# Two S4D convolutions around routed-token layers: the convolution kernel becomes the stationary operand of its spectrum's first stage, ScalarE instead of VectorE moves the result, and D_skip enters by small matmuls

## The chip, the cores and the metric

One NeuronCore of one Trainium2 chip runs the whole program; the other cores are idle. The metric is the device time of one execution in microseconds (us), smaller is better. The engines are named as in the profile: PE (TensorE; PEld is its weight loading), DVE (VectorE), ACT (ScalarE), POOL (GpSimd) and SP (SyncE, whose queue issues nearly all DMAs). Each engine takes its own instructions strictly in the order in which the program lists them, and waits at an instruction until the semaphores that it needs have come.

## What is computed

Four layers follow each other, with residual connections: a convolution layer A, a routed layer B, A again and B again. The sequence has L = 2048 positions and D = 512 channels, all in float32. A is a diagonal state-space model. It builds for each channel a kernel K of 2048 taps out of N = 128 complex states, and convolves the normalized input with it by FFT:

```python
dt = jnp.exp(log_dt)
A = -jnp.exp(log_A_real) + 1j * A_imag
C = (C_real + 1j * C_imag) * dt[:, None]
P = jnp.exp((A * dt[:, None])[:, :, None] * pos[None, None, :])
K = 2.0 * jnp.einsum("dn,dnl->dl", C, P).real
Kf = jnp.fft.rfft(K, 2 * L)
Uf = jnp.fft.rfft(u_t, 2 * L)
y = jnp.fft.irfft(Uf * Kf, 2 * L)[:, :, :L]
return y + u * D_skip
```

Both A layers have the same parameters, so K and its spectrum are computed once. B sends two tokens of the sequence through a SwiGLU network and leaves the rest as it is.

## The kernel before

The channels go in 4 chunks of 128. The kernel K is made in 32 steps of 16 channels, 8 steps for each chunk; `KStep` (L434) is such a step, and `slot(t)` (L722) writes out one slot of a software pipeline in which five steps are under way at a time. In a slot, POOL computes integer phases (`phase`, L454) and decays (`decay`, L465 and L467) by doubling, ACT turns phases into sines and cosines (`trig`, L474 to L476), and DVE and POOL multiply the decays into them (`products`, L482 to L489). PE then contracts over the 128 states (`contract`, L497): 32 matmuls with 32 stationary columns and 64 moving ones fill the PSUM tile `pk`, with 4 channel groups `g` side by side in four column strips of the array. A float32 matmul shows in the profile as two instructions. ACT copies `pk` to the SBUF tile `kt` (L499).

The first stage of K's spectrum is a transform over the 32 coarse positions of each tap, and it is here that the change works. `spectrum` (L501) first adds D_skip to tap 0 of 16 channels by a 128x4 instruction of DVE (L503), out of a tile `dskt` that has a value in partitions 0, 32, 64 and 96 and zeros elsewhere. Then 8 matmuls (L507) hold the constant `d1k` stationary (64 columns) and move `kt`, read with a stride, so that the result `kq` has frequencies on its partitions and (position, channel) on its free axis. `turn` (L514) brings the positions to the partitions by one DVE instruction that transposes blocks of 32x32 (L517) and writes into `gk`, the chunk's input of the second stage.

The second stage (`kf2`, L533 or L524: `kx`) multiplies `gk` by the constant `w2`, ACT copies the result to `kd` (L540), and SP stores it in DRAM as `kfd` (L542). Beside the pipeline, the first convolution of the chunks that are ready runs: `load` reads `kfd` back (`kf`, L561), `f1` transforms the input (PE `zf` L593, DVE transpose `g` L597), `front` multiplies the spectra (PE `pu` L533, DVE `p` L568), `back` transforms back (PE `pv` L579, ACT `v` L580), `fin_a` and `fin_b` finish (DVE `vt` L638, PE `po` L640, DVE `xc` L647), and `stats` (L653, L654) takes the statistics for the next layer. The table `CONV1` names by hand, in thirds of a slot, where each of these pieces stands in program order.

What sets the order: in the slots from 6 to 31 the program order of DVE, ACT and POOL is kept as written (`ORDER_KERNEL`, L136, by `in_order`, L210). The order of PE's instructions and of SP's DMAs there, and the order of all engines in the opening before slot 6, is chosen by a scheduler that weighs ready times by a model of its own. The opening also holds the setup of the state parameters and the statistics of the first normalization. The buffers of the pipeline come in pairs (`KB` = 2): decays `mg`, phases `ph` and sines `sc` of a step can be begun again only when the step two before has used them up. `mg`'s first column is written by ACT (`decay_init`, L459), which so waits until `products` of the step two before are done. There is one `gk` buffer (tag `bigC`) for all chunks; in slots 9, 17 and 25 the `turn` is therefore held back to the next slot's start.

Of the kernel before, what the change touches and what calls it, by code (L numbers as in the profile page):

```python
# [8 lines left out]
F32 = mybir.dt.float32  # L9
# [5 lines left out]
OP = mybir.AluOpType  # L15
# [14 lines left out]
PP = 2  # L30
# Where each step of the work beside the kernel's pipeline, and of what follows it, stands in program order.
CONV1 = dict(
# [110 lines left out]
def constants():  # L143
# [5 lines left out]
    for s in range(2):  # L149
        for h in range(2):  # L150
            d1[s, h, :, s, h, 0, :] = np.cos(th)
            d1[s, h, :, s, h, 1, :] = -np.sin(th)
    d1k = np.zeros((4, 32, 4, 2, 32))
    for g in range(4):
        d1k[g, :, g, 0, :] = np.cos(th)
        d1k[g, :, g, 1, :] = -np.sin(th)
    d4 = np.zeros((2, 2, 32, 2, 32))
    for h in range(2):
        d4[h, 0, :, h, :] = np.cos(th.T) / 2048.0
        d4[h, 1, :, h, :] = -np.sin(th.T) / 2048.0  # L160
    b = np.arange(64)
# [4 lines left out]
    for h in range(2):  # L166
        sl = slice(32 * h, 32 * h + 32)
        w2[h, 0, :, :, 0, :] = c[sl]
        w2[h, 1, :, :, 0, :] = s[sl]
        w2[h, 0, :, :, 1, :] = -s[sl]  # L170
        w2[h, 1, :, :, 1, :] = c[sl]
    w2 = w2.reshape(128, 32, 128)
# [37 lines left out]
@contextmanager  # L210
def in_order(tc, engines):
    """Instructions traced in the block keep their order on each of these engines."""
    seen = tc.nc.cur_bb.bb.instructions
    n = len(seen)
    yield
    prev = {}
    for i in seen[n:]:
        if i.engine in engines:
            if i.engine in prev:
                dep = mybir.DependencyInfo(mybir.DependencyClass.NoSync, mybir.DependencyReason.DATA)  # L220
                tc.add_manual_dep(i, prev[i.engine].name, dep, reason="in_order")
            prev[i.engine] = i


def build(tc, x, lar, aim, cr, ci, ldt, dsk, wr, wg, wu, wd, d1_h, d1k_h, d4_h, w2_h, w3_h, w3b_h, sm_h, out):
# [6 lines left out]
    with ctx:  # L232
# [39 lines left out]
        d1k = kp.tile([128, 256], F32, name="d1k", tag="d1k")  # L272
        dskt = kp.tile([128, 32, 4], F32, name="dskt", tag="dskt")
        LN2H, LN2L = 0.693145751953125, 1.42860682030941723e-06
# [49 lines left out]
        def setup(c0, c1, room):  # L324
            """Phases and decays of a state's powers: plane k holds those of step 2^(k-1), as (coarse, fine) pairs."""
            n = (c1 - c0) * CH
# [107 lines left out]
        class KStep:  # L434
            """Sixteen channels of the kernel and of its spectrum's first stage, in steps."""

# [54 lines left out]
            def contract(self):  # L491
                pk = psk.tile([128, 4, 64], F32, name=f"pk{self.u}", tag="pk")
                for e in range(4):
                    for k in (1, 0):
                        for g in range(4):
                            t = self.sc[:, k, 4 * g + e, :]
                            T.matmul(pk[32 * g : 32 * g + 32, e, :], t[:, 0:32], t[:, 33:97], start=k == 1, stop=k == 0, tile_position=(0, 32 * g))  # L497
                self.kt = kp.tile([128, 4, 64], F32, name=f"kt{self.u}", tag="kt", bufs=2)
                A.activation(self.kt, pk, AF.Copy)  # L499

            def spectrum(self):  # L501
                kt = self.kt
                V.tensor_tensor(kt[:, :, 32], kt[:, :, 32], dskt[:, self.u, :], op=OP.add)  # L503
                self.pq = psk.tile([128, 32, 16], F32, name=f"kq{self.u}", tag="kq")
                for g in range(4):
                    for h in range(2):
                        T.matmul(  # L507
                            self.pq[64 * h : 64 * h + 64, :, 4 * g : 4 * g + 4],
                            d1k[:, 64 * g : 64 * g + 64],
                            kt[:, :, 32 - 32 * h : 64 - 32 * h].rearrange("p e b -> p b e"),  # L510
                            start=True, stop=True, tile_position=(0, 64 * h),
                        )

            def turn(self):  # L514
                if self.s == 0:
                    gks[self.c] = new_big(f"gk{self.c}", "C")
                V.transpose(gks[self.c][:, :, 16 * self.s : 16 * self.s + 16].rearrange("p k e -> p e k"), self.pq.rearrange("p b e -> p e b"))  # L517

# [25 lines left out]
        def kf_pair(c, gi):  # L544
            """Spectra of two groups, even k1 on the lower partitions and odd ones on the upper."""
            kf = sb.tile([128, 2, 2, 2, CH], F32, name=f"kf1_{c}_{gi}", tag="kf", bufs=2)
# [157 lines left out]
        nc.sync.dma_start(d1k, d1k_h)  # L704
        G.memset(dskt, 0.0)
        for g in range(4):
            nc.sync.dma_start(dskt[32 * g : 32 * g + 1].rearrange("p s e -> p (s e)"), dsk[g : g + 1, :])
        def merged(chain, lanes, plan):
            """The chain's steps, with those of each lane put in before the step that the plan names."""
            todo = sorted(((p, k, lane) for lane, ps_ in plan.items() for k, p in enumerate(ps_)), key=lambda w: (w[0], w[2], w[1]))  # L710
# [9 lines left out]
        def slot(t):  # L720
            """One step of the kernel's pipeline; other work may come after any of its instructions."""
            def at(k, f, *a):  # L722
# [77 lines left out]
        class Conv:  # L800
            """One chunk of a convolution layer, in steps."""

# [172 lines left out]
        class Routed:  # L975
            """The layer of the two routed tokens, in steps, and the next convolution's start beside it."""

# [23 lines left out]
            def choose(self):  # L1001
                """Statistics, scores, the two tokens and their normalized rows."""
                i, rdt, small, psum = self.i, self.rdt, self.small, self.psum
# [428 lines left out]
```

## Time and profile before

| | |
|---|---|
| Time of the runs | 697.32 us median of 3 (696.2 to 698.96) |
| Span of the profiled execution | 695.2 us |
| Instructions | 14060 |
| Mean granted TensorE clock | 0.882 |
| Bytes moved by DMA | 97.64 MB, 140 GB/s in the mean |

The span runs from the first to the last instruction that the profiler recorded. The first 43 us hold the opening, the pipeline of the 32 steps runs from there to about 389 us, and the rest is the end of the first convolution, the first routed layer, the second convolution and the second routed layer. Lines of the profile give a group of instructions by source line, engine and operation, `out<-in` by the names of the tiles, the shape, and either the times of one group or the start and length of single pieces. What stands in brackets behind a piece is the time for which its engine had been idle, and what ended that.

### The profile page before, as it was taken

What the parts mean: (1) busy time and instruction counts of PE and PEld (TensorE: products, weight loads), DVE (VectorE), ACT (ScalarE), POOL (GpSimd) and SP (SyncE); (2) the same over time, 40 slices, a digit from 0 to 9 for tenths busy, and PEclk for the clock granted to TensorE, in tenths of its full rate; (3) what the DMA queues carried; (4) which work ended last, traced back from release to release, by engine and by line L of the source; (5) the groups of instructions that cost most, each with busy time, mean ns of one, the idle gap of its engine ahead of it and who ended that gap; (6) DMA issues with size and microseconds to landing.
All of it is one profiled execution on the core that took longest, in us unless ns stands there. A gap on an engine that the chain in (4) does not pass through costs nothing.

```text
span 695.2 us, 14060 instructions
## 1 busy us (share of the span) xinstructions
PE 485.8 (70%) x5300; PEld 360.2 (52%) x5300; DVE 580.9 (84%) x1164; ACT 311.1 (45%) x587; POOL 500.4 (72%) x659
## 2 busy tenths in 40 slices
PE   1012433798988898979789987267799888888336
PEld 1001322577855786648776665034678565656112
DVE  7899998687899999989999964985356799999950
ACT  4445645456753647527473121321511615214272
POOL 4879999999999999987993083260257766757252
PEclk9999775699998989979999998769599899999858
DMA  7961204768410977109460699600813748438436
GB/s 212 225 150 72 90 30 144 262 195 234 118 33 28 218 214 171 53 16 245 117 172 2 184 307 345 164 2 11 178 55 86 154 103 176 145 98 239 108 79 180
DMA packets 51709, 97.64 MB, mean 140 GB/s; under 512 B 4885, under 2 KB 35513, under 8 KB 47161
## 3 DMA queue, kind: packets, MB, share of 16 engines
q1 hardware_dynamic: 51512, 96.72, 51.5%
q8 instruction: 42, 0.69, 0.4%
q14 instruction: 27, 0.21, 0.1%
q0 software_dynamic: 128, 0.02, 0.0%
HBM read 70.23 MB, written 26.48 MB: 139 GB/s over the span
## 4 chain that ended last, share of the span: by engine, by line
DVE 33%; POOL 21%; DMA 16%; PE 14%; issue 8%; SPq 6%; ACT 1%; POOLq 0%; DVEq 0%; ACTq 0%
POOL mg L465 6%; DVE vt L638 6%; POOL ph L454 6%; PE zf L593 4%; DVE g L597 3%; DMA x<-in_x 3%; DVE jn L654 3%; DMA xw<-xs 3%; DVE p L609 3%; SPq L561 3%; DMA kf<-kfd 3%; DMA x<-xs 3%; POOL sc L482 2%; POOL ml L467 2%; DVE p L568 2%
## 5 line engine op out<-in xcount | busy, mean ns | idle before, releaser
L465 POOL TENSOR_TENSOR mg<-mg,pf 128x128 f32<-128x128 f32 (+4 forms) x160 | 108.6, 682 | 5.4 <-ACT pf L423 3.1
L454 POOL TENSOR_TENSOR ph<-ph,pi 128x512 int32<-128x512 int32 (+4 forms) x160 | 112.0, 702 | 0.5
L497 PE MATMUL pk<-sc 128*32 128x64 f32 x2048 | 46.3, 247 | 74.2 <-DVE sc L489 63.5
L618 POOL TENSOR_TENSOR y<-p 64x256 f32<-64x256 f32 x76 | 55.9, 736 | 50.0 <-DVE p L609 35.6
L507 PE MATMUL kq<-kt,d1k 128*64 128x128 f32 x512 | 63.4, 402 | 30.8 <-DVE kt L503 22.5
L593 PE MATMUL zf<-z,d 128*128 128x256 f32 x256 | 80.1, 453 | 5.9 <-DVE g L597 5.1
L497 PEld LDWEIGHTS pk<-sc 128*32 128x32 f32 x2048 | 38.4, 126 | 87.8 <-issue 57.8
L638 DVE STREAM_TRANSPOSE vt<-v 128x512 f32<-128x512 f32 x64 | 69.2, 1098 | 3.3 <-ACT v L626 2.5
L597 DVE STREAM_TRANSPOSE g<-zf 128x512 f32<-128x512 f32 x64 | 65.9, 1051 | 7.0 <-PE zf L593 7.0
L626 ACT ACTIVATE v<-pv 128x512 f32<-128x512 f32 x40 | 23.7, 596 | 97.9 <-PE pv L625 97.9
L593 PEld LDWEIGHTS zf<-z,d 128*128 128x128 f32 x256 | 52.7, 222 | 24.9 <-DVE g L597 11.7
L507 PEld LDWEIGHTS kq<-kt,d1k 128*64 128x64 f32 x512 | 40.1, 159 | 46.7 <-DVE kt L503 25.2
L640 PE MATMUL po<-vt,d 128*64 128x256 f32 x256 | 45.0, 432 | 23.1 <-DVE vt L638 22.6
L619 POOL TENSOR_TENSOR y<-p 64x256 f32<-64x256 f32 x76 | 55.6, 731 | 4.6
L625 PE MATMUL pv<-y,w 128*128 128x128 f32 x320 | 54.8, 302 | 5.0 <-POOL y L619 3.7
L524 PE MATMUL pu<-g,w 128*64 128x128 f32 x640 | 50.2, 298 | 10.2 <-DVE g L1297 3.6
L489 DVE TENSOR_TENSOR sc<-mg,sc 128x1024 f32<-128x1024 f32 x32 | 57.3, 1790 | 0.0
L625 PEld LDWEIGHTS pv<-y,w 128*128 128x128 f32 x320 | 45.1, 201 | 19.6 <-POOL y L619 9.5
L482 POOL TENSOR_TENSOR sc<-mg,sc 128x512 f32<-128x512 f32 x25 | 40.8, 1631 | 12.3 <-ACT sc L476 12.3
L609 DVE TENSOR_TENSOR p<-pu,kf 128x1024 f32<-128x1024 f32 x32 | 38.4, 1209 | 12.8 <-PE pu L524 6.2
L524 PEld LDWEIGHTS pu<-g,w 128*64 128x64 f32 x640 | 38.7, 147 | 18.4 <-DVE p L609 6.2
L579 PE MATMUL pv<-p,w 128*128 128x128 f32 x192 | 40.7, 296 | 7.5 <-DVE p L568 7.1
(344 smaller groups left out, 1175.0 us busy)
## 6 DMA issues: line engine op xcount, KB each, us to landing
kf<-kfd SPq DMA_DIRECT2D x144, 128.0 KB, 4.0
kfd<-kd SPq DMA_DIRECT2D x16, 512.0 KB, 6.8
wd<-in_wd SPq DMA_DIRECT2D x4, 1792.0 KB, 14.0
w<-in_w SPq DMA_DIRECT2D x2, 2048.0 KB, 11.1
x<-in_x SPq DMA_DIRECT2D x8, 512.0 KB
xc<-in_x SPq DMA_DIRECT2D x8, 512.0 KB, 6.0
z<-in_x SPq DMA_DIRECT2D x8, 512.0 KB, 6.4
xs<-xc SPq DMA_DIRECT2D x8, 512.0 KB, 4.3
```

The lines of the kernel that those rows point to most:

```text
L454: G.tensor_tensor(self.ph[:, :, n : 2 * n], self.ph[:, :, 0:n], self.step_of(self.pis, k + 1, n), op=OP.add)
L465: G.tensor_tensor(mg[:, :, n : 2 * n], mg[:, :, 0:n], self.step_of(self.pfs, k + 1, n), op=OP.mult)
L489: V.tensor_tensor(sc[:, :, :, at], m.rearrange("p (o d) i -> p o d i", o=1).to_broadcast([128, 2, 16, 32]), sc[:, :, :, at], op=OP.mult)
L497: T.matmul(pk[32 * g : 32 * g + 32, e, :], t[:, 0:32], t[:, 33:97], start=k == 1, stop=k == 0, tile_position=(0, 32 * g))
L507: T.matmul(self.pq[64 * h : 64 * h + 64, :, 4 * g : 4 * g + 4], d1k[:, 64 * g : 64 * g + 64], kt[:, :, 32 - 32 * h : 64 - 32 * h].rearrang ...
L524: T.matmul(pt[64 * par : 64 * par + 64, ri, q, :], w2[:, k1, 64 * ri : 64 * ri + 64], src[:, k1, :], start=True, stop=True, tile_position= ...
L593: T.matmul(pf[:, 16 * s : 16 * s + 16, :], d1[:, 128 * s : 128 * s + 128], z[:, :, 16 * q : 16 * q + 16], start=True, stop=True)
L597: V.transpose(g[:, :, 16 * q : 16 * q + 16].rearrange("p k e -> p e k"), pf.rearrange("p b e -> p e b"))
L609: V.tensor_tensor(pp, pu.rearrange("p (o r) q e -> p o r (q e)", o=1).to_broadcast([128, 2, 2, 2 * CH]), kf.rearrange("p r (o q) e -> p r ...
L618: E.tensor_tensor(y[0:64, :, par, :], p1[ls, 0], p2[ls, 1], op=OP.subtract)
L625: T.matmul(pv[:, k, :], w3[:, 4 * gi + k, :], y[:, k // 2, k % 2, :], start=True, stop=True)
L638: V.transpose(vt.rearrange("p b e -> p e b"), v[:, :, es].rearrange("p k e -> p e k"))
```

## The change

`contract` adds D_skip on PE: between the two passes over a column of `pk` it puts 4 matmuls of 4 contraction rows, 32 stationary columns (of the constant tile `sm`, of which only column 0 of each strip holds a one) and 1 moving column, which add to tap 0. So L497's 32 matmuls of a step become 48. The DVE addition (L503) goes. `dskt` is now 4 partitions high, loaded by one DMA in place of four, and its clearing by POOL goes.

`spectrum` swaps the operands: `kt` (64 columns, contiguous) is stationary, `d1k` (128 columns, contiguous) moves, and there are 8 matmuls as before. The result has the positions on its partitions already, so `turn` needs no transpose; it is a copy of the 128x512 result by ACT, written into `gk` with a step of 128 elements (512 bytes) from one element to the next. To suit the new order of partitions (real and imaginary part outside, half of the positions inside), the constants `d1`, `d1k`, `d4` and `w2` are permuted, in their values only; no shape of their use changes.

```diff
-        dskt = kp.tile([128, 32, 4], F32, name="dskt", tag="dskt")
+        dskt = kp.tile([4, 32, 4], F32, name="dskt", tag="dskt")
...
             def contract(self):
                 pk = psk.tile([128, 4, 64], F32, name=f"pk{self.u}", tag="pk")
                 for e in range(4):
-                    for k in (1, 0):
+                    for k in (1, None, 0):
                         for g in range(4):
-                            t = self.sc[:, k, 4 * g + e, :]
-                            T.matmul(pk[32 * g : 32 * g + 32, e, :], t[:, 0:32], t[:, 33:97], start=k == 1, stop=k == 0, tile_position=(0, 32 * g))
-                self.kt = kp.tile([128, 4, 64], F32, name=f"kt{self.u}", tag="kt", bufs=2)
-                A.activation(self.kt, pk, AF.Copy)
+                            at, gs = pk[32 * g : 32 * g + 32, e, :], (0, 32 * g)
+                            if k is None:
+                                T.matmul(at[:, 32:33], sm[0:4, 200 + 32 * g : 232 + 32 * g], dskt[:, self.u, e : e + 1], start=False, stop=False, tile_position=gs)
+                            else:
+                                t = self.sc[:, k, 4 * g + e, :]
+                                T.matmul(at, t[:, 0:32], t[:, 33:97], start=k == 1, stop=k == 0, tile_position=gs)
+                self.kt = kp.tile([128, 4, 2, 32], F32, name=f"kt{self.u}", tag="kt", bufs=2)
+                A.activation(self.kt, pk.rearrange("p e (h b) -> p e h b", h=2)[:, :, ::-1, :], AF.Copy)
 
             def spectrum(self):
-                kt = self.kt
-                V.tensor_tensor(kt[:, :, 32], kt[:, :, 32], dskt[:, self.u, :], op=OP.add)
-                self.pq = psk.tile([128, 32, 16], F32, name=f"kq{self.u}", tag="kq")
-                for g in range(4):
-                    for h in range(2):
+                self.pq = psk.tile([128, 4, 4, 32], F32, name=f"kq{self.u}", tag="kq")
+                for e in range(4):
+                    for ri in range(2):
                         T.matmul(
-                            self.pq[64 * h : 64 * h + 64, :, 4 * g : 4 * g + 4],
-                            d1k[:, 64 * g : 64 * g + 64],
-                            kt[:, :, 32 - 32 * h : 64 - 32 * h].rearrange("p e b -> p b e"),
-                            start=True, stop=True, tile_position=(0, 64 * h),
+                            self.pq[64 * ri : 64 * ri + 64, e].rearrange("p g k -> p (g k)"),
+                            self.kt[:, e].rearrange("p h b -> p (h b)"),
+                            d1k[:, 128 * ri : 128 * ri + 128],
+                            start=True, stop=True, tile_position=(0, 64 * ri),
                         )
 
             def turn(self):
                 if self.s == 0:
                     gks[self.c] = new_big(f"gk{self.c}", "C")
-                V.transpose(gks[self.c][:, :, 16 * self.s : 16 * self.s + 16].rearrange("p k e -> p e k"), self.pq.rearrange("p b e -> p e b"))
+                A.activation(
+                    gks[self.c][:, :, 16 * self.s : 16 * self.s + 16].rearrange("p k (g e) -> p e g k", g=4),
+                    self.pq, AF.Copy)
...
-        G.memset(dskt, 0.0)
-        for g in range(4):
-            nc.sync.dma_start(dskt[32 * g : 32 * g + 1].rearrange("p s e -> p (s e)"), dsk[g : g + 1, :])
+        nc.sync.dma_start(dskt.rearrange("p s e -> p (s e)"), dsk)
```

The tables of the program order (`CONV1` and the others) are as before. The scheduler, which sees other instructions, lists some of the rest in another order: in the opening the last steps of DVE's chain that doubles the decays (L426) stand behind statistics of the input (L788); where the second stage of chunk 0 begins, SP's queue has the load of the next input `z` ahead of the stores of `kfd`, and for chunks 1 and 2 the four loads of the first `kf` ahead of the second store of `kfd`, where each stood behind; and PE has `kq` earlier at several places, that of steps 15 and 23 ahead of a finishing tile `po` and three tiles `zf` of the input's transform, where it stood behind them. From the routed layer on, all engines have the same order as before.

More of the change, by code (lines that the diff above doesn't have):

```diff
@@ L150, in constants @@
         for h in range(2):
-            d1[s, h, :, s, h, 0, :] = np.cos(th)
-            d1[s, h, :, s, h, 1, :] = -np.sin(th)
-    d1k = np.zeros((4, 32, 4, 2, 32))
+            d1[s, h, :, s, 0, h, :] = np.cos(th)
+            d1[s, h, :, s, 1, h, :] = -np.sin(th)
+    d1k = np.zeros((4, 32, 2, 4, 32))
     for g in range(4):
-        d1k[g, :, g, 0, :] = np.cos(th)
-        d1k[g, :, g, 1, :] = -np.sin(th)
+        d1k[g, :, 0, g, :] = np.cos(th)
+        d1k[g, :, 1, g, :] = -np.sin(th)
     d4 = np.zeros((2, 2, 32, 2, 32))
     for h in range(2):
-        d4[h, 0, :, h, :] = np.cos(th.T) / 2048.0
-        d4[h, 1, :, h, :] = -np.sin(th.T) / 2048.0
+        d4[0, h, :, h, :] = np.cos(th.T) / 2048.0
+        d4[1, h, :, h, :] = -np.sin(th.T) / 2048.0
     b = np.arange(64)
@@ L167, in constants @@
         sl = slice(32 * h, 32 * h + 32)
[L168 to L171, printed above, removed]
+        w2[0, h, :, :, 0, :] = c[sl]
+        w2[1, h, :, :, 0, :] = s[sl]
+        w2[0, h, :, :, 1, :] = -s[sl]
+        w2[1, h, :, :, 1, :] = c[sl]
     w2 = w2.reshape(128, 32, 128)
```

## The prediction

> **What bounds the kernel now.** I read the engines' totals first, then busy time by stage, then what ended the idle time of the engine that is busy throughout a stage.
>
> ```profile
> PE 485.8 (70%) x5300; PEld 360.2 (52%) x5300; DVE 580.9 (84%) x1164; ACT 311.1 (45%) x587; POOL 500.4 (72%) x659
> ```
>
> The totals name DVE, but the change lies in the pipeline of the 32 steps alone, 43 to about 389 us. The view by windows (busy us of PE, PEld, DVE, ACT, POOL, each with its count) shows who fills it:
>
> ```profile
> 43.00:200.00 157.00, 94.17 (x1408) 77.53 (x1408) 136.86 (x160) 89.65 (x146) 155.50 (x175) 0.84 0.44 138
> 200.00:300.00 100.00, 85.72 (x1142) 65.16 (x1140) 97.68 (x141) 55.13 (x91) 98.67 (x126) 0.93 0.46 119
> 300.00:376.00 76.00, 67.13 (x862) 53.67 (x864) 72.65 (x112) 43.35 (x72) 62.67 (x83) 0.92 0.48 126
> 376.00:400.00 24.00, 22.28 (x272) 15.74 (x268) 23.66 (x63) 2.78 (x5) 0.20 (x1) 1.00 0.48 137
> ```
>
> Up to 300 us POOL is busy 254 of 257 us: whatever DVE sheds there cannot shorten the stage, because POOL's own 32 steps of phases, decays and products are untouched. From 200 us on DVE is full as well (97.68 of 100), and after 300 us POOL falls to 62.67 of 76: something keeps it waiting. The timeline of POOL has these pieces with idle time ahead of them:
>
> ```profile
> 310.30 0.29 POOL L465 TENSOR_TENSOR mg<-mg,pf 128x32 f32<-128x32 f32 x1 [1.52 <-ACT mg L459]
> 320.93 1.99 POOL L482 TENSOR_TENSOR sc<-mg,sc 128x512 f32<-128x512 f32 x1 [4.52 <-ACT sc L476]
> 350.78 1.77 POOL L482 TENSOR_TENSOR sc<-mg,sc 128x512 f32<-128x512 f32 x1 [0.96 <-ACT sc L476]
> 373.32 1.21 POOL L482 TENSOR_TENSOR sc<-mg,sc 128x512 f32<-128x512 f32 x1 [4.54 <-ACT sc L476]
> ```
>
> Together 11.54 us, all of it on ACT's cosines or first columns. ACT is not full (43.35 of 76); its queue stands. The timelines of ACT, DVE and PE before the second of those gaps say for whom:
>
> ```profile
> 309.95 0.27 ACT L459 ACTIVATE mg<-pf 128x32 f32<-128x32 f32 x1 [6.01 <-DVE sc L489]
> 314.25 0.60 ACT L540 ACTIVATE kd<-kx 128x512 f32<-128x512 f32 x1 [4.03 <-PE kx L533]
> 319.66 1.19 ACT L476 ACTIVATE sc<-ph,cst 128x1056 f32<-128x1056 f32 x1
> ```
>
> ```profile
> 307.76 0.29 DVE L503 TENSOR_TENSOR kt<-kt,dskt 128x4 f32<-128x4 f32 x1
> 308.58 1.28 DVE L489 TENSOR_TENSOR sc<-mg,sc 128x1024 f32<-128x1024 f32 x1
> 311.89 1.11 DVE L517 STREAM_TRANSPOSE gk<-kq 128x512 f32<-128x512 f32 x1 [1.10 <-PE kq L507]
> ```
>
> ```profile
> 304.75 5.18 PE L593 MATMUL zf<-z,d 128*128 128x256 f32 x12
> 309.86 1.98 PE L507 MATMUL kq<-kt,d1k 128*64 128x128 f32 x16
> ```
>
> ACT stood 6.01 us because DVE came late to its products, and 4.03 us because `kx` needs `gk`, which needed the transpose (311.89), the matmuls `kq` (309.86) and the addition (307.76), all waiting in DVE's and PE's queues. So a full DVE reaches POOL through ACT. That is the chain which the change cuts.
>
> **The change part by part.** The groups that it touches, or that are like what it adds (busy us, mean ns of one):
>
> ```profile
> L517 DVE STREAM_TRANSPOSE gk<-kq 128x512 f32<-128x512 f32 x32 | 34.5, 1079 | 2.3 <-PE kx L533 1.2 <-PE kq L507 1.1
> L503 DVE TENSOR_TENSOR kt<-kt,dskt 128x4 f32<-128x4 f32 x32 | 14.1, 442 | 8.8 <-ACT kt L499 8.8
> L540 ACT ACTIVATE kd<-kx 128x512 f32<-128x512 f32 x32 | 18.4, 594 | 33.7 <-PE kx L533 14.5 <-PE kx L524 10.8 <-DVE p L609 5.4
> ```
>
> 1. DVE loses 1.08 + 0.44 = 1.52 us a step, 48.6 us in all. About 20 steps of it fall where POOL alone sets the pace (to 300 us) and are worth nothing by themselves, but they let DVE catch up with POOL. In 300 to 376 us about 8 steps fall: 12.2 us less of DVE's 72.65. Bounds of what reaches the end: 0 (POOL's gaps stay) to the 11.54 us of gaps, since POOL's 62.67 us of work remain. Both limits agree on 11 to 12 us; I take 10, as ACT keeps other waits.
>
> 2. ACT gains the copy. The nearest row is L540 (128x512 out of PSUM, 0.594 us), the far one the transpose itself (1.079 us, the same scattered write); 19.0 to 34.5 us in all, I take 0.6 us a step. It is hidden in ACT's idle time (32.6 us of 76). Without this cover, each step would be 0.6 us longer. The copy waits for `kq`; behind it in ACT's queue stand the `kt` copy of the next step, the `kd` and `v` copies, and the next slot's sines, for which POOL waits. But just ahead of it stands L459, which waits for DVE's products of the same slot anyway, and `kq` no longer waits for DVE. Cost 0 here, and a rival below.
>
> 3. PE's `kq`: 16 instructions take 1.98 us with strided operands. The same shape with contiguous ones is this piece:
>
> ```profile
> 392.69 1.09 PE L524 MATMUL kx<-gk,w 128*64 128x128 f32 x16
> ```
>
> So 0.89 us less a step (bounds 0 and 0.89). The 16 small matmuls are 32 instructions between those of `pk`, in another tiling of the array (32x32 in 128x32). How dear that is shows where `pk` is broken up by `po`:
>
> ```profile
> 372.16 0.64 PE L497 MATMUL pk<-sc 128*32 128x64 f32 x26
> 372.73 0.65 PE L640 MATMUL po<-vt,d 128*64 128x256 f32 x4
> 373.31 0.31 PE L497 MATMUL pk<-sc 128*32 128x64 f32 x6
> 373.56 0.65 PE L640 MATMUL po<-vt,d 128*64 128x256 f32 x4
> 381.72 1.10 PE L497 MATMUL pk<-sc 128*32 128x64 f32 x64
> ```
>
> Unbroken, 64 take 1.10 us or 0.017 each; broken, 26 take 0.57 to the next start (0.45 at that pace) and 6 take 0.25 (0.10): 0.12 to 0.15 us for a switch. A switch lies between 0 (should the next weights be in) and 0.15; I take 0.1. Eight switches a step and 32 instructions at 0.017: 0.8 + 0.54 = 1.3 us more, bounds 0.5 and 1.7. With `kq`, +0.4 us a step (-0.4 to +1.7). In 300 to 376 us, 8 steps make 3 us (-3 to +14) on PE's 67.13 of 76, of which 9 are free: cost 0 to the end at the taken value, and 5 us beyond its room at the far one, a rival.
>
> On this the Trainium skill speaks against the change: TensorEngine Tiling (Array Packing), section Tiling Modes, says that changing the tiling mode drains the array. The broken `pk` agrees that there is a price. By a whole passage for each switch, the mean length of a `pk` matmul in the row below, it would be 8 x 0.25 = 2.0 us a step in place of 0.8, and the sum of PE +1.6 in place of +0.4.
>
> ```profile
> L497 PE MATMUL pk<-sc 128*32 128x64 f32 x2048 | 46.3, 247 | 74.2 <-DVE sc L489 63.5 <-POOL sc L486 7.5 <-DVE sc L486 2.5
> ```
>
> 4. The end of the pipeline, 376 to 400 us, is DVE's (23.66 of 24) and PE's (22.28):
>
> ```profile
> 384.17 1.01 DVE L517 STREAM_TRANSPOSE gk<-kq 128x512 f32<-128x512 f32 x1
> 388.48 1.01 DVE L517 STREAM_TRANSPOSE gk<-kq 128x512 f32<-128x512 f32 x1
> ```
>
> Two transposes and two additions (0.26) go, 2.3 us; PE's 1.7 us of slack bounds the gain. I take 2 (0 to 2.3).
>
> 5. The opening. Four DMAs of `dskt` become one and a clearing of POOL goes; POOL's last two waits before its full stretch are
>
> ```profile
> 4.05 1.20 SPq L707 DMA_DIRECT2D dskt<-in_dsk  x4
> 37.26 1.19 POOL L482 TENSOR_TENSOR sc<-mg,sc 128x512 f32<-128x512 f32 x1 [2.27 <-ACT sc L476]
> 41.74 1.31 POOL L359 TENSOR_TENSOR su_bigB<-su_w,su_bigB 128x384 f32<-128x384 f32 x1 [1.86 <-DVE su_bigB L358]
> ```
>
> The inputs are asked for 0.9 us sooner. In the new order POOL does phases first, while DVE's later doublings wait for statistics, and meets DVE's L358 with more work already behind it. Between 4.1 us won (both waits) and 3 lost (waits of this kind anew); I take 1 won.
>
> 6. SP's queue. For chunks 1 and 2 the loads of the first `kf` wait for the first store to land, and the second store is now behind them:
>
> ```profile
> 235.19 2.58 SPq L561 DMA_DIRECT2D kf<-kfd  x4
> ```
>
> ```profile
> 230.38 4.74 DMA kfd<-kd
> ```
>
> ```profile
> 242.74 1.20 ACT L476 ACTIVATE sc<-ph,cst 128x1056 f32<-128x1056 f32 x1
> 249.17 1.24 POOL L482 TENSOR_TENSOR sc<-mg,sc 128x512 f32<-128x512 f32 x1
> ```
>
> The second row is from the chain of waits: a store lands 4.74 us after its issue. So the second store goes out 5 to 6 us later, its buffer is free later, and ACT's third pair of `kd` copies waits for it with the sines behind. POOL has some 5 us in hand at chunk 1 (cosine done at 243.94, its user L482 at 249.17), less at chunk 2. 0 to 5 us; I take 2 lost.
>
> 7. The permuted constants change no instruction: 0. POOL itself may run a little faster: the addition, which reads two SBUF tiles as POOL's work does, took 0.44 us in the mean, but 0.12 while POOL stood:
>
> ```profile
> 379.12 0.12 DVE L503 TENSOR_TENSOR kt<-kt,dskt 128x4 f32<-128x4 f32 x1
> ```
> If each held POOL up for 0.12, 3.8 us; I take 0.
>
> Sum against the profiled execution: 10 + 2 + 1 - 2 = 11 us off 695.2, a span of 684.2. The runs' median, 697.3, lies 2.1 us above the span: **686.3 us**. Its own range, from the bounds of items 1 and 4 to 6 taken mostly one at a time, is 680 to 693.
>
> **The rivals.** (a) *The gaps come back.* ACT's other waits (for `pv`, `pk`, `kx`) take the place of those on DVE; only items 4 and 5 remain: 697.3 - 3 = 694.3, with 1 or 2 us of item 6 against it up to 696. For it: three of the four gaps are 1 us and more on cosines, which only ACT makes. Against: DVE's lateness stood at the root.
>
> (b) *ACT becomes the queue that decides*, on the other side. The copy waits for PE in order, and PE's queue holds `kq` behind tiles that wait for DVE; each time the sines behind it come later than POOL wants them. The margin is already gone where a gap of 0.96 us stands (350.78). The three waits for L476 cost 10.0 us, 3.3 each; if from 200 us on every second step (9 of 17) meets one, 30 us, 20 more than now, less 3 of items 4 and 5: 714. With every third step, 20 us: 704. It decides from the point where `kq` ends later than L459. Against: `kq` leaves DVE's queue.
>
> (c) *PE becomes the bound.* At +1.7 us a step, 17 steps from 200 us make 29 us on PE's 152.9 of 176: 5.8 us too much, none of the 10 us gained, and 3 won elsewhere: 700. By the drained passage of the Trainium skill's page (above), with `kq` saving nothing, it would be 2.5 a step, 43 us, 20 beyond the room: 714. For it: PE is the fullest engine after DVE at the end. Against: `kq`'s strided operands are plainly what makes it slower than L524.
>
> (d) *Everything runs through*: all gaps, the whole of items 4 and 5 and POOL's 3.8: 11.5 + 2.3 + 4.1 + 3.8 = 21.7 us, 676.
>
> **How the numbers follow.** Forecast 0.55, (a) 0.14, (b) 0.15, (c) 0.11, (d) 0.05. What a measurement can tell from no change is 0.5%, 693.8 to 700.8 us. Forecast and (d) are faster, and a little of (a), 0.62; most of (a) and of the lower half of (c) the same, 0.15; the rest slower, 0.23. The range 679 to 704 takes in (a), (c)'s first price and the milder (b); it leaves out (d) and the dearer prices, under 2 in 10.
>
> **What would show it.** Right: POOL's gaps of 4.5 us at 321 and 373 gone, DVE under 90% busy from 200 us, `kq` near 1.1 us, the copy near 0.6 us, and the last `gk` written some 12 us sooner. Item 3 wrong: `pk` beyond 2.8 us. (b): POOL waits for ACT's cosines while ACT waits for `kq`. (c): PE over 95% busy from 200 us. Wrong altogether: POOL's pieces themselves longer, or the pipeline not full at 43 us.

## The result, and the profile after

The changed kernel takes 706.28 us (median of 4 runs, 702.17 to 707.44) beside 697.69 us of the kernel before on the same chip: a ratio of 1.0118, 95% interval 1.0079 to 1.0157. It is slower by 1.2%, where 1.6% faster was forecast. The profiled execution took 707.44 us, with a span of 705.7.

The totals of the engines on the page of the kernel after:

```profile
PE 507.1 (72%) x6324; PEld 382.9 (54%) x6324; DVE 532.8 (76%) x1100; ACT 337.5 (48%) x619; POOL 494.7 (70%) x658
```

DVE lost the 48 us of busy time that the prediction took from it, ACT gained 26 and PE 21. By stages (the windows of the prediction; columns: busy us of PE, PEld, DVE, ACT, POOL, then granted clock, DMA share and GB/s):

```profile
43.00:200.00 157.00, 106.75 (x1837) 86.21 (x1838) 118.15 (x140) 97.60 (x154) 155.66 (x176) 0.82 0.43 138
200.00:300.00 100.00, 89.54 (x1382) 73.13 (x1380) 78.36 (x119) 64.27 (x101) 85.62 (x118) 0.91 0.48 119
300.00:376.00 76.00, 68.63 (x1081) 58.28 (x1080) 61.48 (x96) 45.46 (x76) 66.81 (x85) 0.91 0.48 126
```

To 200 us nothing has changed for POOL: it is as full as before. From 200 to 300 us DVE fell from 97.68 to 78.36, as it should, but POOL fell with it, from 98.67 to 85.62. The engine that set the pace now waits, and no engine is full. The timeline of POOL after 200 us says for what (the larger gaps; in brackets the idle time ahead and what ended it):

```profile
208.13 1.20 POOL L482 TENSOR_TENSOR sc<-mg,sc 128x512 f32<-128x512 f32 x1 [1.23 <-ACT sc L476]
242.03 2.24 POOL L482 TENSOR_TENSOR sc<-mg,sc 128x512 f32<-128x512 f32 x1 [5.88 <-ACT sc L476]
294.94 1.20 POOL L482 TENSOR_TENSOR sc<-mg,sc 128x512 f32<-128x512 f32 x1 [2.04 <-ACT sc L476]
327.94 1.53 POOL L482 TENSOR_TENSOR sc<-mg,sc 128x512 f32<-128x512 f32 x1 [5.44 <-ACT sc L476]
380.19 1.20 POOL L482 TENSOR_TENSOR sc<-mg,sc 128x512 f32<-128x512 f32 x1 [4.43 <-ACT sc L476]
```

The gaps that were to go came back in greater number, and still on ACT's cosines: 21.6 us in seven waits from 43 to 390 us, 10.0 in three before. ACT itself has 35 of 100 us free; what it waits for, and what PE does in the changed lines, stands in the waits of ACT from 43 to 390 us (total us, times, longest) and in the groups by line (busy us, mean ns of one; idle time before them):

```profile
ACT v L585 <- PE pv L584: 33.3, 12, 5.0
ACT kt L503 <- PE pk L501: 18.7, 12, 4.2
ACT gk L520 <- PE kq L510: 2.9, 2, 2.4
```

```profile
L520 ACT ACTIVATE gk<-kq 128x512 f32<-128x512 f32 x32 | 33.9, 1058 | 5.0 <-PE kq L510 5.0
L498 PE MATMUL pk<-dskt,sm 4*32 4x1 f32 x1024 | 32.8, 182 | 0.0
```

ACT's new copy (L520) takes 1.06 us and waits for little. What ACT waits for are PE's old results, `pv` and `pk`. In the kernel before it waited for `pk` even longer:

```profile
ACT kt L499 <- PE pk L497: 32.2, 19, 7.6
```

So these totals alone accuse nobody; what has changed on PE must say more. One step's `kq` and `pk` on PE's timeline of the kernel after:

```profile
192.24 1.09 PE L510 MATMUL kq<-d1k,kt 128*64 128x128 f32 x16
193.26 0.32 PE L501 MATMUL pk<-sc 128*32 128x64 f32 x8
193.51 0.24 PE L498 MATMUL pk<-dskt,sm 4*32 4x1 f32 x8
193.68 0.43 PE L501 MATMUL pk<-sc 128*32 128x64 f32 x16
194.04 0.24 PE L498 MATMUL pk<-dskt,sm 4*32 4x1 f32 x8
...
195.27 0.32 PE L501 MATMUL pk<-sc 128*32 128x64 f32 x8
```

`pk` lasts from 193.26 to 195.59, 2.33 us in place of 1.10 unbroken. `kq` takes 1.09, as predicted. So the suspicion goes to the small matmuls.

### The profile page after: what moved, and what is told of

It is laid out like the page before. It is cut to its first block, busy times and chain, and to the rows that moved or that the text cites. A ratio compares the mean times of both kernels' runs of the same rounds, so it can differ in the third digit from the quotient of the medians.

```text
span 705.7 us, 16088 instructions
## 1 busy us (share of the span) xinstructions
PE 507.1 (72%) x6324; PEld 382.9 (54%) x6324; DVE 532.8 (76%) x1100; ACT 337.5 (48%) x619; POOL 494.7 (70%) x658
## 4 chain that ended last, share of the span: by engine, by line
PE 28%; DVE 27%; DMA 16%; POOL 13%; issue 8%; SPq 5%; ACT 3%; POOLq 0%; DVEq 0%; ACTq 0%
PE pv L584 5%; DVE vt L643 4%; PE pk L501 4%; DVE g L602 4%; PE zf L598 4%; POOL ph L454 3%; DVE jn L659 3%; DMA xw<-xs 3%; POOL mg L465 3%; DMA x<-xs 3%; DVE p L614 3%; DMA xc<-in_x 3%; DMA x<-in_x 3%; DMA kf<-kfd 3%; PE kx L538 2%
## 5 line engine op out<-in xcount | busy, mean ns | idle before, releaser
L501 PE MATMUL pk<-sc 128*32 128x64 f32 x2048 | 72.2, 251 | 64.5 <-DVE sc L489 56.1
L454 POOL TENSOR_TENSOR ph<-ph,pi 128x64 int32<-128x64 int32 (+4 forms) x160 | 111.9, 702 | 3.6 <-ACT ph L448 3.4
L465 POOL TENSOR_TENSOR mg<-mg,pf 128x512 f32<-128x512 f32 (+4 forms) x160 | 109.1, 684 | 7.3 <-ACT pf L423 6.1
L598 PE MATMUL zf<-z,d 128*128 128x256 f32 x256 | 75.4, 430 | 13.1 <-DVE g L602 7.1
L501 PEld LDWEIGHTS pk<-sc 128*32 128x32 f32 x2048 | 42.0, 122 | 75.5 <-issue 62.0
L598 PEld LDWEIGHTS zf<-z,d 128*128 128x128 f32 x256 | 49.1, 209 | 29.0 <-DVE g L602 12.3
L573 DVE TENSOR_TENSOR p<-pu,kf 128x1024 f32<-128x1024 f32 x24 | 28.9, 1218 | 43.2 <-PE pu L538 21.5
L510 PE MATMUL kq<-d1k,kt 128*64 128x128 f32 x512 | 42.7, 320 | 22.2 <-ACT kt L503 22.2
L482 POOL TENSOR_TENSOR sc<-mg,sc 128x512 f32<-128x512 f32 x25 | 36.4, 1455 | 21.6 <-ACT sc L476 21.6
L510 PEld LDWEIGHTS kq<-d1k,kt 128*64 128x64 f32 x512 | 34.8, 162 | 29.4 <-ACT kt L503 24.9
L614 DVE TENSOR_TENSOR p<-pu,kf 128x1024 f32<-128x1024 f32 x32 | 38.4, 1209 | 11.3 <-PE pu L529 4.7
## 6 DMA issues: line engine op xcount, KB each, us to landing
x<-in_x SPq DMA_DIRECT2D x8, 512.0 KB, 10.4
```

Of the source, the lines that this page charges most:

```text
L454: G.tensor_tensor(self.ph[:, :, n : 2 * n], self.ph[:, :, 0:n], self.step_of(self.pis, k + 1, n), op=OP.add)
L465: G.tensor_tensor(mg[:, :, n : 2 * n], mg[:, :, 0:n], self.step_of(self.pfs, k + 1, n), op=OP.mult)
L501: T.matmul(at, t[:, 0:32], t[:, 33:97], start=k == 1, stop=k == 0, tile_position=gs)
L510: T.matmul(self.pq[64 * ri : 64 * ri + 64, e].rearrange("p g k -> p (g k)"), self.kt[:, e].rearrange("p h b -> p (h b)"), d1k[:, 128 * ri ...
L598: T.matmul(pf[:, 16 * s : 16 * s + 16, :], d1[:, 128 * s : 128 * s + 128], z[:, :, 16 * q : 16 * q + 16], start=True, stop=True)
L614: V.tensor_tensor(pp, pu.rearrange("p (o r) q e -> p o r (q e)", o=1).to_broadcast([128, 2, 2, 2 * CH]), kf.rearrange("p r (o q) e -> p r ...
```

## The experiments

Two theories at first. *P*: the small matmuls on PE make the loss, as `pk` is 1.2 us longer in every step. *A*: ACT makes it, with a copy of 1.06 us ahead of the sines. Every time is given as a ratio to the kernel before, measured on the same chip in the same session, with its 95% interval; 1% is 7.0 us.

**e1_no_dskip.** The small matmuls left out, with nothing in their place:

```
-                    for k in (1, None, 0):
+                    for k in (1, 0):
```

> The changed kernel without D_skip: the small matmuls are left out and nothing takes their place, so the output lacks the term D_skip * x. Theory P (PE's small matmuls: pk 1.1 to 2.3 us a step, everything behind them on PE late): the pk matmuls are back at about 1.1 us a step, and the time falls to 690 to 698 us. Theory A (ACT's queue: the scattered copy of 1.06 us a step, with its waits, makes the sines late): the copy is as before, POOL still waits some 20 us for ACT's sines, and the time stays at 703 to 707 us. If both have a part, it lies between.

Measured: 0.9931 (0.9902 to 0.9959), median 691.48 us; POOL has no wait in the pipeline. Theory P's range; the copy on ACT is still there. All that the change loses came with the small matmuls, and without them the rest of it gains. But leaving them out also let the scheduler choose another order, so this run does not yet say whether their execution or that order costs.

**e2_small_alone.** The small matmuls put into the kernel before, DVE's addition taken out:

```
-                    for k in (1, 0):
+                    for k in (1, None, 0):
...
-                V.tensor_tensor(kt[:, :, 32], kt[:, :, 32], dskt[:, self.u, :], op=OP.add)
```

> The kernel before with one part of the change: D_skip enters by the 16 small matmuls a step, DVE's addition is gone; old orientation, transposes on DVE. Theory P: PE is 1.2 us a step later, the DVE addition saves 0.44 us a step on an engine that was full; the time is 702 to 708 us. Theory A: ACT's queue is the old one, so no loss; DVE's relief gives a little, 692 to 698 us.

Measured: 1.0197 (1.0165 to 1.0229), 710.05 us, beyond P's range: put into the kernel before, the small matmuls cost 2%, although an addition of 0.44 us a step left a full DVE. PE's order changed here too (its sequence of tiles on the timeline differs from the kernel before at some thirty places), so the 2% is execution and order together.

**e3_turn_on_dve.** ACT's part undone:

```
-                A.activation(gks[self.c][...].rearrange("p k (g e) -> p e g k", g=4), self.pq, AF.Copy)
+                V.tensor_copy(gks[self.c][...].rearrange("p k (g e) -> p e g k", g=4), self.pq)
```

> The changed kernel with one part undone: DVE in place of ACT moves kq into gk, as a plain copy with the same scattered write. Theory A: ACT is as free as before, and POOL's waits for the sines fall from 20 us to 10; 695 to 700 us. Theory P: PE's queue is unchanged, so 704 to 709 us, and DVE over 90% busy from 200 us on.

Measured: 1.0163 (1.0137 to 1.0190), 708.19 us. P's range in time; theory A falls. DVE was not over 90%, but at 88.5% from 200 to 300 us. PE's order is close to that of the changed kernel, but not the same.

**e4_same_tiling.** The small matmuls with all 128 rows, in the tiling of their neighbours:

```
-  T.matmul(at[:, 32:33], sm[0:4, 200 + 32 * g : 232 + 32 * g], dskt[:, self.u, e : e + 1], ...)
+  T.matmul(at[:, 32:33], sm[:, 200 + 32 * g : 232 + 32 * g], dskt[:, self.u, e : e + 1], ...)
...
-        dskt = kp.tile([4, 32, 4], F32, name="dskt", tag="dskt")
+        dskt = kp.tile([128, 32, 4], F32, name="dskt", tag="dskt")
```

> The changed kernel, with the small matmuls in the tiling of those around them (128 rows by 32 columns: the stationary operand has all 128 partitions, zero outside row g, and so has the moving one, cleared once by POOL): as many instructions, no change of tiling. Theory P with the switch as its price: pk takes 1.5 to 1.7 us a step instead of 2.3 and the time falls to 697 to 702 us. Theory P with the instructions themselves as the price: pk stays at 2.2 or more and the time at 704 to 708. Theory A: 704 to 707 whatever pk takes.

Measured: 1.0069 (1.0040 to 1.0097), runs from 697 to 708 us. `pk` fell to 1.36 us, nearly all of the added time gone, yet the loss over e1 was still 1.4%. So P alone does not account for it. What the two also differ in is the order that the scheduler gives PE and SP: e4 has exactly that of the changed kernel, e1 another. This made a second pair of theories: *X*, the small matmuls cost by being executed, and *O*, by the order which the scheduler chose with them there.

**e9_after_in_e1_order and e10_e1_in_after_order.** Each engine is held to the order of the other kernel, by a chain of dependencies without a semaphore from each instruction to the next in a list:

```
+            for x in todo:
+                for i in [big[x]] + after.get(x, []):
+                    if prev is not None:
+                        tc.add_manual_dep(i, prev.name, dep, reason="in_order")
+                    prev = i
```

> Every instruction of the changed kernel, the small matmuls too, held on all five engines to the order that the instructions have in e1_no_dskip (each four small ones right behind the k = 1 matmuls that they follow in the program). Theory X (the small matmuls cost by being executed: pk 1.2 us longer, late on PE): 703 to 708 us, as the changed kernel. Theory O (they cost by the other order into which the scheduler put PE, SP and the opening around them): 690 to 697 us. Both: between.

> The reverse: e1_no_dskip (no small matmuls and no D_skip term in the output) held to the order that the instructions have in the changed kernel. Theory X: 689 to 696 us, as e1_no_dskip. Theory O: 701 to 707 us, with POOL's waits for ACT's sines of 10 us and more in the pipeline. Both: between.

Measured: e9 1.0023 (0.9992 to 1.0054), e10 1.0042 (1.0018 to 1.0066). With 699.80 us e9 lies between the two ranges, with 701.65 us e10 lies in theory O's. Both theories have a part. e10 executes no small matmul, and its POOL waits for the cosines all the same (waits of POOL from 43 to 380 us):

```profile
POOL sc L511 <- ACT sc L505: 17.1, 6, 5.2
```

**e11_same_tiling_e1_order and e12_same_tiling_after_order.** The small matmuls of e4 in each of the two orders.

> The small matmuls of e4_same_tiling (128 rows by 32 columns, no change of tiling) in the order of e1_no_dskip: pk some 1.4 us a step instead of 1.1 and 2.3. Theory X: a quarter of the loss remains, 693 to 698 us. Theory O: 690 to 693. If this one and e9 lie together above 700, it is the instructions and not the switches.

> The small matmuls without change of tiling, in the order of the changed kernel. If that order costs its 10 us by itself, as e10_e1_in_after_order says: 699 to 703 us. If it costs only together with something the small matmuls do: 690 to 694.

Measured: e11 0.9876 (0.9822 to 0.9930), median 690.02 us; e12 1.0060 (1.0029 to 1.0092), a repeat of e4, whose order was the same already, and within its interval. Both lie in the ranges that theory O gave.

**e17_two_switches.** The small matmuls as in the change, but gathered, in e1's order (`start` only with the first of a bank, `stop` only with the last):

```
-                for e in range(4):
-                    for k in (1, None, 0):
+                for k in (1, None, 0):
+                    for e in range(4):
```

> e9_after_in_e1_order (699.8 us) with the 16 small matmuls of a step gathered between all k = 1 and all k = 0 matmuls of pk: the same small matmuls in the same other tiling, 2 changes of tiling a step in place of 8. If the changes are the price (0.9 us a step by the difference of pk between 2.3 and 1.4): pk some 1.6 to 1.7 us and 690 to 695 us. If the small matmuls of 4 rows are themselves slow: pk 2.2 us and more, 698 to 702.

Measured: 0.9921 (0.9884 to 0.9958), and a step's `pk` on its timeline:

```profile
190.47 0.66 PE L530 MATMUL pk<-sc 128*32 128x64 f32 x32
191.05 0.43 PE L527 MATMUL pk<-dskt,sm 4*32 4x1 f32 x32
191.41 0.66 PE L530 MATMUL pk<-sc 128*32 128x64 f32 x32
```

1.60 us from 190.47 to 192.07. The same matmuls of 4 rows, gathered, add 0.50 us to `pk` in place of 1.23, and nothing to the end that the intervals could show: the price is the change of tiling. Gathering also moves all passes of k = 1 ahead of those of k = 0; no run gathers without the small matmuls, so what that alone is worth is not known. The two causes side by side (`pk` at full granted clock):

| small matmuls in a step | `pk` of a step | in e1's order | in the order of the changed kernel |
|---|---|---|---|
| none | 1.10 us | e1 0.9931 | e10 1.0042 |
| 16, same tiling | 1.36 us | e11 0.9876 | e12 1.0060 |
| 16, two switches | 1.60 us | e17 0.9921 | not run |
| 16, eight switches | 2.33 us | e9 1.0023 | the change, 1.0118 |

Down a column is what execution costs: the eight switches 0.9% over none in e1's order and 0.8% in the other. Along a row is what the order costs: 0.95 to 1.8%. Each cause taken alone from e1, 0.92 for the one and 1.11 for the other, makes 2.0% in sum, and the two together make 1.9%. From e11, with the same tiling, it is 1.5 and 1.8, 3.3% in sum, against 2.4 together. So both causes stand, with sizes near 1% each; that they simply add is not shown.

**e13_only_sp_order and e14_only_pe_order.** e1 with one queue alone in the other order.

> e1_no_dskip (691.5 us; no D_skip term) with SP's DMAs alone in the order of the changed kernel, PE, DVE, ACT and POOL in its own. If SP's order (kf loads ahead of the second kfd store, the weights' loads at the end) is what costs 10 us in e10_e1_in_after_order: 698 to 702 us. If it is PE's: 690 to 693.

> e1_no_dskip (no D_skip term) with PE's matmuls alone in the order of the changed kernel. If PE's order (pk, kx, kq and pu of neighbouring steps placed otherwise) is what costs 10 us: 698 to 702 us. If it is SP's or the opening's: 690 to 693. If both queues share it, each gives 694 to 697.

Measured: e13 0.9945 (0.9909 to 0.9980), e14 1.0009 (0.9967 to 1.0051), its runs spread from 692 to 706 us. PE's order alone makes 0.8% of e10's 1.1%; SP's 0.1%, which the intervals do not tell from nothing. The medians make SP's part larger: e14's, 700.79 us, lies in the range that PE's order as the cause was to give, and e13's, 696.01, in neither range of its own, 4.5 us above e1's. In the profiled execution of e13 (696.91 us) POOL waits 10.7 us for cosines, in that of e1 not at all. So a part of SP's is not ruled out.

**e7_add_on_dve and e8_operands_only.** The way without small matmuls: DVE adds D_skip, as before, to the new layout; in e8 DVE copies as well.

```
+                V.tensor_tensor(self.kt[:, :, 0, 0], self.kt[:, :, 0, 0], dskt[:, self.u, :], op=OP.add)
```

> The changed kernel with D_skip put in by DVE's addition of four columns, as before; the rest of the change (operands of kq swapped, ACT moves the result) stays. If the small matmuls, by execution or by order, are the whole loss, the time is that of e1_no_dskip plus what DVE's 0.44 us a step cost on an engine with some 12 us free of 100: 691 to 696 us. If DVE's part on the way from pk to kq matters as much as PE's, 696 to 702.

> e7_add_on_dve (691.8 us) with DVE moving kq into gk too, as a plain copy: of the whole change only the swapped operands of kq are left, DVE does per step what it did before. If DVE's relief is what the change wins: 695 to 699 us, as before. If the shorter kq is what it wins: 690 to 694.

Measured: e7 0.9894 (0.9842 to 0.9945), 691.84 us; e8 0.9972 (0.9942 to 1.0002), the same as before. The windows of e7 and then e8:

```profile
200.00:300.00 100.00, 79.62 (x1149) 61.86 (x1148) 93.66 (x138) 66.56 (x104) 98.67 (x126) 0.93 0.46 119
300.00:376.00 76.00, 65.01 (x949) 54.69 (x950) 68.79 (x110) 48.76 (x78) 69.13 (x83) 0.92 0.50 126
```

```profile
200.00:300.00 100.00, 79.35 (x1081) 63.48 (x1079) 97.80 (x138) 54.51 (x90) 95.85 (x127) 0.91 0.48 119
300.00:376.00 76.00, 65.32 (x921) 55.09 (x922) 74.13 (x116) 43.42 (x72) 60.53 (x82) 0.87 0.48 126
```

e7 lies in the range for the small matmuls as the whole loss, e8 in the range for DVE's relief. PE has the tiles in e8 in the same sequence as in the kernel before, so e8 comes nearest to the shorter `kq` alone: it brings nothing that the interval could show. With the shorter `kq` alone DVE stays full (third figure, 97.80) and POOL (fifth) idles; with the move to ACT DVE has room and POOL runs full to 300 us and does 69.13 us of work in 300 to 376, 8.6 more. e7 has another order of PE than e8, so a part of their difference may be order.

Three of these versions compute the whole output and beat both kernels: e11, 1.24% faster than before, e7, 1.06%, and e17, 0.79%.

## Why the prediction was wrong

**Two steps failed. The first is the last half of item 3**: the small matmuls "make 3 us on PE's 67.13 of 76, of which 9 are free: cost 0 to the end at the taken value"; their switches cost 0.8 to 0.9%, 5 to 6 us. **The second is item 6**, which prices SP's new order alone, and with it item 1, which takes 10 us of gaps as won: in the order that the changed kernel got, the gaps stay even without a small matmul (e10), and that order costs 1.1%, 8 us. Together they turn the 4.8 us that the rest of the change won in e1 into a loss of 8.6 us. That the rest won 4.8 us and not the forecast 11 has to do with what lies behind the last `gk` (below).

Item 3's price on PE was right as a sum, and its own sign of being wrong, `pk` beyond 2.8 us, did not appear: the sign looked at the price, not at who waits. It took 1.3 us a step more for `pk` (2.33 − 1.10 = 1.23 measured), 0.89 less for `kq` (1.98 − 1.09), 0.4 net (0.34). In its parts it was off both ways, which is luck: 0.8 for the switches (0.97 measured, 2.33 − 1.36) and 0.54 for the instructions themselves (0.26, 1.36 − 1.10). The price of one switch follows from PE's timeline of e11, against the same rows of the kernel after, shown above:

```profile
201.12 0.32 PE L530 MATMUL pk<-sc 128*32 128x64 f32 x8 [0.88 <-POOL sc L515]
201.25 0.22 PE L527 MATMUL pk<-dskt,sm 128*32 128x1 f32 x8
201.31 0.41 PE L530 MATMUL pk<-sc 128*32 128x64 f32 x16
201.54 0.22 PE L527 MATMUL pk<-dskt,sm 128*32 128x1 f32 x8
```

Eight instructions of small matmuls pass in 0.06 us here (201.25 to 201.31) and in 0.17 with the change of tiling (193.51 to 193.68); sixteen of `pk` in 0.23 (201.31 to 201.54) and 0.36 (193.68 to 194.04). That is 0.11 and 0.13 us a switch, eight of them 0.96 a step. e17's two switches add 0.24 us to `pk` (1.60 − 1.36), 0.12 each. The Trainium skill, TensorEngine Tiling (Array Packing), section Tiling Modes, says that changing the mode drains the array. The trace agrees that it costs, at half of the 2.0 us a step that the prediction made of that sentence.

What failed is the setting of 9 us of PE's idle time against it. Idle time of PE is where PE waits for a product or for `kt`; the added 1.2 us stands elsewhere, between the products and `kt`, with `kt`, `kd` and `v` of ACT, and behind them the sines, waiting for it in order. The waits of ACT for `pk` from 43 to 390 us, in e1, then e11, then e9, all three in the same order (in kernels held to an order the line numbers are 29 higher, since the list stands ahead):

```profile
ACT kt L503 <- PE pk L501: 5.8, 6, 3.5
```

```profile
ACT kt L532 <- PE pk L530: 7.5, 8, 3.7
```

```profile
ACT kt L532 <- PE pk L530: 17.9, 14, 4.4
```

e11 and e9 differ in the small matmuls' tiling (and in the zeros that pad them) alone: with the switches ACT waits 10.4 us more for `pk`, POOL waits 7.9 us for cosines where it waits for none in e11, the last `gk` begins at 383.20 us in place of 376.85, and e9 is 1.5% slower. So a small work on a busy engine reaches the end not through the engine's throughput but through a queue that stands behind one of its results. That `pk` is the whole of this way is argued; the granted clock has a part in it (below). From 200 to 300 us POOL is as full in e9 as before (98.67 of 100) and all its waits come after 300 us: its fall to 85.62 in the changed kernel goes with the order (89.64 in e10).

**What the prediction left out: the scheduler.** Item 6 counted SP's new order, but not PE's, although the text ahead of the prediction says that `kq` comes earlier at several places. The rows of one place show how PE's order delays the sines. Near 197 us, PE's timeline of e1,

```profile
196.48 0.39 PE L584 MATMUL pv<-p,w3b 128*128 128x128 f32 x2
196.79 1.10 PE L510 MATMUL kq<-d1k,kt 128*64 128x128 f32 x16
197.82 0.49 PE L584 MATMUL pv<-p,w 128*128 128x128 f32 x2
...
199.71 1.03 PE L598 MATMUL zf<-z,d 128*128 128x256 f32 x4
```

has one group of `pv` ahead of this `kq`, the second straight behind it, and `zf` behind both. In e10, with the same work in the order of the changed kernel,

```profile
195.38 1.09 PE L539 MATMUL kq<-d1k,kt 128*64 128x128 f32 x16
196.40 0.49 PE L613 MATMUL pv<-p,w 128*128 128x128 f32 x2
...
198.29 1.89 PE L627 MATMUL zf<-z,d 128*128 128x256 f32 x8
200.02 0.38 PE L613 MATMUL pv<-p,w 128*128 128x128 f32 x2
```

`kq` stands ahead of both groups and eight `zf` between them, and ACT, which has its `v` copies ahead of the sines, comes to the sines at 202.50 instead of 200.40. ACT's timeline in e1 and in e10:

```profile
199.91 0.60 ACT L585 ACTIVATE v<-pv 128x512 f32<-128x512 f32 x1 [2.41 <-PE pv L584]
200.40 1.09 ACT L474 ACTIVATE sc<-ph 128x1056 f32<-128x1056 int32 x1
```

```profile
202.01 0.60 ACT L614 ACTIVATE v<-pv 128x512 f32<-128x512 f32 x1 [2.92 <-PE pv L613]
202.50 1.09 ACT L503 ACTIVATE sc<-ph 128x1056 f32<-128x1056 int32 x1
```

The granted clock from 186 to 196 us differs too, 0.66 in e10 and 0.83 in e1, so the delay is not the order's alone. POOL has no gap here yet: its product of these cosines (ready at 205.94) begins at 206.01. Its first wait in e10, 4.81 us, ends at 238.86, behind cosines that stood in ACT's queue behind `kd` copies waiting for `kx`. That this order costs about 1% is shown by e10 and e14. Through which places it costs that is argued from the trace: the places were not tried one by one.

**What no run takes apart: the granted clock.** At that wait, and at others, PE ran slowly. Here are 24 matmuls `kx`, for whose result ACT's `kd` copies wait, with the sines behind them, in the changed kernel, e9 and e11:

```profile
230.42 5.31 PE L538 MATMUL kx<-gk,w 128*128 128x128 f32 x24
```

```profile
307.63 5.48 PE L567 MATMUL kx<-gk,w 128*128 128x128 f32 x24
```

```profile
304.07 2.94 PE L567 MATMUL kx<-gk,w 128*128 128x128 f32 x24
```

The granted clock was 0.50 in the first two stretches (229 to 235 and 307 to 313 us) and 1.00 in the third (304 to 307). POOL's next waits for cosines are the 5.88 us of the list above and 3.04 us in e9, none in e11. So up to some 2.4 us of each wait can hang on the clock. In e1, e7, e11 and e17, whose POOL has no such wait, these `kx` take 2.94 us at both places. In e12, POOL waits 3.09 us (to 323.51) behind `kx` of 2.94, so the clock is not the whole. Whether order and switches brought the low clock to this place, or whether it fell there in the profiled execution by chance, no run shows. The mean clock of a run does not decide: 0.863 in e11's run of 689.32 us, 0.864 in e12's of 703.23.

Point by point, the rest of the sum:

- **Item 1 was right as a term, but only in another order.** Where the switches and the order are gone, POOL's gaps are gone, all of them. e11 from 200 us on, and its last `gk`:

```profile
200.00:300.00 100.00, 81.90 (x1492) 65.78 (x1491) 88.16 (x130) 69.22 (x107) 98.67 (x126) 0.97 0.47 119
300.00:376.00 76.00, 63.04 (x1198) 53.96 (x1198) 65.20 (x103) 47.34 (x77) 67.69 (x82) 0.96 0.48 127
376.00:400.00 24.00, 21.94 (x270) 17.68 (x267) 18.61 (x61) 6.28 (x11) 8.18 (x13) 1.00 0.91 275
```

```profile
376.85 1.05 ACT L549 ACTIVATE gk<-kq 128x512 f32<-128x512 f32 x1 [2.70 <-PE kq L539]
```

  The last `gk` is written at 377.90, where the transpose before ended at 389.49: 11.6 us sooner, "some 12" in the prediction. DVE is under 90%, POOL at 98.67. In the changed kernel the same write starts at 392.83 and ends at 393.91.
- **What happens behind the last `gk` was left out**: the prediction took for granted that what is won or lost there reaches the end as it is. The span follows it only in part:

| | before | e11 | after |
|---|---|---|---|
| last `gk` written | 389.49 us | 377.90 | 393.91 |
| load `xc` landed | 419.44 us | 408.65 | 424.61 |
| last copy `v` of the first convolution begun | 430.41 us | 422.06 | 438.57 |
| span | 695.2 us | 688.7 | 705.7 |

  The load is a piece of the chain that ended last, in the kernel before, in e11 and after; about it the DMA engines are full (share 0.99 to 1.01 over some 30 us from 390, 380 and 395 us):

```profile
406.07 13.37 DMA xc<-in_x
```

```profile
391.95 16.70 DMA xc<-in_x
```

```profile
405.80 18.81 DMA xc<-in_x
```

  Up to its landing e11 keeps 10.8 of its 11.6 us, and the changed kernel is 5.2 us late. Behind it e11 gives back 4.3 us, and the changed kernel loses another 5.3, half of its 10.5. So the pipeline, which the experiments are about, explains no more than half of the longer span of this execution directly. From the last `gk` to the end it is 305.7 us before, 311.8 after, and 310.6 to 311.6 in e1, e7, e9, e10 and e11 as well, with or without the switches (the others lie between 307.3 in e2 and e8 and 316.1 in e17, each by one profiled execution). Why is open.
- **Item 2** had the copy at 0.6 us; it takes 1.06, the far bound (the transpose's 1.08). The plain copy with the same scattered write takes 1.05 on DVE in e3, so the transposing is not the price. It was hidden all the same: e7 and e8 say that the move is worth 0.8%, with the difference of their orders in it.
- **Item 6** took 2 us; SP's order alone gave 1 by the ratios of e13 and e1, within intervals that reach from a gain to about 4. The wait that was foreseen, ACT's `kd` copies for the store of `kfd`, is in e13, 16.1 us in four waits from 43 to 390 us, the first of them at chunk 0:

```profile
158.24 1.09 ACT L574 ACTIVATE kd<-kx 128x512 f32<-128x512 f32 x2 [5.03 <-DMA kfd<-kd]
```

- **Items 4, 5 and 7** cannot be read apart: POOL is full from 43 us in both kernels, as assumed.

Of the rivals, (a) had the mechanism of the second failed step: in e10 the gaps come back on ACT's waits for PE (38.7 us for `pv`, 17.2 for `kx`, 14.1 for `pk`), but (a) let them cost no more than before, 694 to 696 us. (b) had the size (704 to 714) and the visible sign, POOL waiting for L476, but not the cause: ACT's copy waited 2.9 us for `kq` and could be moved to DVE without gain. (c) had the cause of the first, the small matmuls, but asked for a full PE; 89.54 of 100 was enough. The range ended at 704: (b) and (c) were priced apart, and the dearer part of both was left out.

## What to carry to other kernels

Idle time of an engine pays for added work only if the work can slide into it; ask instead which in-order queues wait for the result that the work delays, and what stands behind those waits. A few tiny matmuls of another tile size can cost more (here 1.23 us a step) than is won by making the reads of large ones contiguous (0.89): keep the tile size of the neighbours by padding with zero rows, or gather them. Where a scheduler orders an engine, a changed instruction changes the order of others; holding two kernels to each other's order tells the two effects apart. Where a piece of PE's work takes twice its usual time, look at the granted clock of its stretch before calling the order the cause.

## What the runs showed of the hardware

A change of tiling between matmuls cost 0.11 to 0.13 us on this chip, against 0.06 us for eight instructions of small matmuls in the tiling of their neighbours (e11). A copy of 128x512 out of PSUM took 1.06 us on ACT and 1.05 on DVE when each element landed 512 bytes from the last, 0.6 on ACT with contiguous ones (`kd`): on ACT the way of writing decided. No DVE copy of this size with contiguous writes was there to compare. The same 24 matmuls took 2.94 us at a granted clock of 1.00 and 5.31 to 5.48 at 0.50.
